# First group in 64-row transposes and 128x64 product tiles, state products moved, and other homes and queue places for the weight pieces of an mLSTM + SwiGLU kernel

## The chip, the cores and the metric

The kernel runs on one core of one Trainium2 chip. The metric is the device time of one execution in microseconds (us).

## The reference

An mLSTM cell over 4 batches, 8 heads, 768 steps and head size 40, then a SwiGLU feed-forward block over the 3072 resulting tokens (320 features, 1536 hidden):

```python
for t in range(S):                      # per batch and head
    m_new  = maximum(f[t] + m, i[t])
    f_stab, i_stab = exp(f[t] + m - m_new), exp(i[t] - m_new)
    C = f_stab * C + i_stab * outer(v[t], k[t])
    n = f_stab * n + i_stab * k[t]
    y[t] = sigmoid(o[t]) * (C @ q[t]) / maximum(abs(n @ q[t]), 1)
x   = y as (B*S, H*D) = (3072, 320)
out = (silu(x @ w_gate) * (x @ w_val)) @ w_out
```

q, k, v, the gates and the output are float32. The three weight matrices reach the kernel as 64-bit floats, so that a weight is two 32-bit words in DRAM.

## The kernel before, in words

**Groups.** The 768 steps are cut into six groups of 128 tokens (for 4 batches a group is 512 tokens). Group 0 has no earlier state and is computed in a form of its own (the functions named `first_...`). Later groups work in half groups of 64 tokens with a state `C` kept in `C_ring`. The core runs group 0's cell, then the feed-forward of group 0 while the cell of group 1 is prepared between its blocks, and so on.

**Order.** The scheduling is manual: every engine executes its instructions in the order in which the program writes them, and waits where an input or a buffer is not ready. That holds for DMA issues too: `nc.sync.dma_start` stands in SyncE's order (SP in the profile), `nc.scalar.dma_start` in ScalarE's (ACT). A wait therefore holds up all that stands behind it on the same engine. `A`, `V` and `G` stand for ScalarE, VectorE (DVE) and GpSimd (POOL).

**Group 0's cell (lines 599 to 646).** The heads are handled in two halves P = 0 and 1 (two batches u each). The decay weights of the first 128 steps are built in PSUM by three rounds of matmuls (L512, L516, L521) and go through Exp into `W0` (a view of `h_sb[:, 0:8]`). `first_turn` transposes k and q (128x128 tiles, L541), `first_scores` multiplies them (L551) and DVE multiplies the scores into `W0` (L555). `first_own(u)` multiplies `W0` with the values (L562), `first_x` divides by the normaliser, `sig` applies Sigmoid to the output gate `o_sb` on ACT, `first_gate` multiplies it in. `first_seam` transposes x into `xT` for the feed-forward (L596), and `first_state` (L584) makes the state that group 1 starts from. `burn` (L501) is matmuls without use. PSUM tiles come from two rings of four banks each, "cell" and "gen".

**Weight pieces.** `PIECES` numbers ten loads, p0 to p9. p0 and p1 hold the gate and value weights of one block of 128 hidden features, p2 to p6 those of two blocks (p2: blocks 2 and 3, ... p5: 8 and 9, p6: 10 and 11), each in three DMAs: one for the gate half (640 KB in p2 to p6) and two for the value half (512 and 128 KB). p7 to p9 hold `w_out`, 1280 KB each, in blocks 12 to 17. `piece_load` puts the raw words into a buffer of the ring `raw` (two buffers) or into a borrowed home. `convert(j)` turns a block into float32 in three steps: `scale(j)` (two ACT instructions, L211 and L213), `join(j)` (two DVE instructions, L220 and L221), and `rounded(j)` (L228, on POOL or DVE).

**Feed-forward of group 0.** `hidden(0, m)` is one block of 128 hidden features: 20 matmuls (`gv_ps`, L683), then the conversions that `ahead[m]` names, then Silu on ACT (L688) and a product on DVE (L689) that frees the two PSUM banks. Those matmuls use two of the four "gen" banks, so that block m + 2 needs the product of block m to be done. `ahead` converts block j at an earlier m: block 7 and 8 at m = 5, 9 at 6, 10 at 7, 11 at 8. After block m the functions in `slots[m]` are called: the loads of group 1's k, q, v, the sums over the later gates (`late_sums`, `late_maxima`, `late_decay`), a store of the maxima `M_sb` to a DRAM tile `M_dram`, and `weights_load(1)`, two loads of `M_dram` spread over partitions into `w_sb`. From slot 7 on `w_sb` becomes group 1's decay weights: `weights_sub` on DVE (L483), `weights_mask` on POOL (L488), `weights_exp` on ACT (L492), then the product with the scores (`weigh`, L359) and the state sums on TensorE (`add`, L378).

The core of `hidden`, which sets the order of steps that the change leaves alone:

```python
for kc in range(NKC): ...               # 20 matmuls L683
for f in first:                         # the conversions of ahead[m]
    f()
nc.scalar.activation(sg, ps[0], AF.Silu)
nc.vector.tensor_tensor(hid(g, m), sg, ps[1], op=ALU.mult)
```

Of the kernel before, what the change touches and what calls it, by code (L numbers as in the profile page):

```python
# [14 lines left out]
ALU = mybir.AluOpType  # L15
# [9 lines left out]
def kernel(  # L25
# [50 lines left out]
    def bank(name, tag="cell"):  # L76
        return psum.tile([128, 512], F32, name=name, tag=tag)
# [61 lines left out]
    def copy(eng, dst, src):  # L139
        if eng is nc.scalar:  # L140
            nc.scalar.copy(dst, src)
        else:
            eng.tensor_copy(dst, src)
# [16 lines left out]
    def piece_load(p, home=None):  # L160
        kind, m, n = PIECES[p]
        if kind == "gv":
            a, d = NKC, n * 128
            gate_w, val_w = (w[:, m * 128:(m + n) * 128].rearrange("(c p) f -> p c f", p=HP) for w in (moe_w_gate, moe_w_val))
            src = [(slice(0, HP), slice(0, NKC), gate_w), (slice(HP, 128), slice(0, NKC - 1), val_w[:, 1:]),
                   (slice(HP, 128), slice(NKC - 1, NKC), val_w[:, 0:1])]
            queues = (nc.sync,) + 2 * (nc.scalar if p < 5 else nc.sync,)
        else:
            a, d = n, DM
            src = [(slice(0, 128), slice(0, n), moe_w_out[m * 128:(m + n) * 128].rearrange("(a p) d -> p a d", p=128))]  # L170
            queues = (nc.sync,)
        if src[0][2].dtype == F32:
            for r, cs, w in src:
                if kind == "o":
                    nc.sync.dma_start(out=wo_sb[r, m:m + n, :], in_=w)
                else:
                    for x in range(n):
                        nc.sync.dma_start(out=wgv_sb[r, m + x, cs], in_=w[:, :, ts(x, 128)])
            return
        if home is None:  # L180
            raw = conv.tile([128, 4 * NKC * 128], U32, name="raw")
        else:
            raw = home.rearrange("p a t -> p (a t)").bitcast(U32)
        raw = raw[:, 0:2 * a * d]
        for (r, cs, w), queue in zip(src, queues):
            queue.dma_start(out=raw[r].rearrange("p (a d) -> p a d", a=a)[:, cs], in_=w.bitcast(U32))
        words = raw.rearrange("p (a d two) -> p a d two", two=2, a=a)
        raws[p] = (words[:, :, :, 0], words[:, :, :, 1])
        split(p)
# [40 lines left out]
    def convert(j, eng=None):  # L230
        scale(j)
        join(j)
        rounded(j, eng)
# [41 lines left out]

    M0 = early.tile([128, L], F32)
    M_of = wo_sb.rearrange("p m d -> p (m d)")[:, 0:H * L].rearrange("p (h t) -> p h t", t=L)
    M_sb = early.tile([BH, NS - 2, SUB], F32)
    m_in = early.tile([BH, NS - 2, 1], F32)
    step1 = keep1  # L280
# [13 lines left out]
    def late_sums():  # L294
        nc.vector.tensor_tensor_scan(flat(f_sb), flat(keep1), flat(f_sb), 0.0, op0=ALU.mult, op1=ALU.add)
        nc.gpsimd.memset(step1, 0.0)
        nc.gpsimd.tensor_sub(i_sb, i_sb, f_sb)
# [11 lines left out]
    M_dram = tc.dram_tile([BH, S - L], F32, name="M_dram")  # L309


    def turn_one(P, src, dst, engs):
        tp = [bank("tp_kq").rearrange("p (a t) -> p a t", t=SUB) for _ in range(2)]
        for a in range(UA):
            h = P * UH + 2 * a
            for i in range(2):
                nc.tensor.transpose(tp[i][:, a, :], src[half(i), h:h + 2, :].rearrange("p h d -> p (h d)"),
                                    ident[half(i), half(i)])
        for i in range(2):
            copy(engs[i], dst[:, P * UA:(P + 1) * UA, half(i)], tp[i])  # L320
# [139 lines left out]
    def xT(n):  # L460
        return xT_sb
# [36 lines left out]
    def burn(n, tag="cell"):  # L498
        t = bank("burn", tag)
        for _ in range(n):  # L500
            nc.tensor.matmul(t, lhsT=junk[:, 0:128], rhs=junk, start=True, stop=True)  # L501
# [29 lines left out]
    def first_values(P):  # L531
        nc.gpsimd.tensor_copy(w_end[:, heads(P)], W0[:, heads(P), end])
        nc.gpsimd.tensor_tensor(vw_sb[:, heads(P)], v_sb[:, heads(P)], w_end[:, heads(P)].to_broadcast([128, UH, D1]),
                                op=ALU.mult)

    def first_turn(P, src, dst, engs):
        for b in range(2):
            tp = bank("tp_kq").rearrange("p (a t) -> p a t", t=L)
            for a in range(UA // 2):
                h = P * UH + b * H + 2 * a  # L540
                nc.tensor.transpose(tp[:, a, :], src[:, h:h + 2, :].rearrange("p h d -> p (h d)"), ident)  # L541
            a = P * UA + b * UA // 2
            copy(engs[b], dst[:, a:a + UA // 2, :], tp)

    def first_scores(P):
        for b in range(2):
            sp = [bank("sp").rearrange("p (a t) -> p a t", t=L) for _ in range(2)]
# [11 lines left out]
    def first_own(u):  # L559
        first_y[u] = bank("first_y", "gen")[:, 0:H * D1].rearrange("p (h d) -> p h d", d=D1)  # L560
        for h in range(H):
            nc.tensor.matmul(first_y[u][:, h, :], lhsT=W0[:, u * H + h, :], rhs=v_sb[:, u * H + h, :], start=True, stop=True)  # L562

    def first_x(u):
        y = first_y.pop(u)
        den = work.tile([128, UH, 1], F32, name="den")[:, 0:H]
        nc.vector.tensor_scalar(den, y[:, :, D:], scalar1=1.0, scalar2=None, op0=ALU.max)
        nc.vector.scalar_tensor_tensor(den, in0=y[:, :, D:], scalar=-1.0, in1=den, op0=ALU.mult, op1=ALU.max)
        nc.vector.reciprocal(den, den)
        nc.vector.tensor_tensor(x_sb[:, u, 0:DM].rearrange("p (h d) -> p h d", d=D), y[:, :, 0:D],  # L570
                                den.to_broadcast([128, H, D]), op=ALU.mult)

    def first_gate(P):
        for u in (2 * P, 2 * P + 1):
            x = x_sb[:, u, 0:DM].rearrange("p (h d) -> p h d", d=D)
            nc.vector.tensor_tensor(x, x, o_sb[:, u * H:(u + 1) * H], op=ALU.mult)
        nc.gpsimd.tensor_copy(x_sb[:, 2 * P:2 * P + 2, DM:], x_sb[:, 2 * P:2 * P + 2, 0:HP])

    def first_state(P, tag="cell"):
# [7 lines left out]
    def first_kept(P, ps, eng):  # L587
        copy(eng, state(2)[:, P * UA:(P + 1) * UA], ps)

    def first_seam(P, engs):  # L590
        for c, eng in zip(range(0, NKC, 2), engs):
            cs = range(c, min(c + 2, NKC))
            tp = bank("tp_x")[:, 0:len(cs) * 2 * L].rearrange("p (c u s) -> p c u s", u=2, s=L)
            for w in cs:
                for b in range(2):
                    nc.tensor.transpose(tp[:, w - c, b, :], x_sb[:, 2 * P + b, ds(w * HP, 2 * HP)], ident)  # L596
            copy(eng, xT(0)[:, c:c + len(cs), 2 * P * L:(2 * P + 2) * L].rearrange("p c (u s) -> p c u s", u=2), tp)

    burn(7)
    banks = [(u, j) for j in range(2) for u in range(B)]  # L600
    for f in (first_mask, first_inputs, first_maxima):
        for u, j in banks:
            f(u, j)
    first_exp(0)
    first_turn(0, k_sb, kT, (V, V))
    first_turn(0, q_sb, qT, (A, V))
    first_exp(1)
    first_values(0)
    first_scores(0)
    first_own(0)  # L610
    late_sums()
    first_turn(1, k_sb, kT, (A, A))
    first_x(0)
    first_turn(1, q_sb, qT, (A, V))
    load(o_sb, o_gate, 0, 1)
    piece_load(0)
    first_own(1)
    first_values(1)
    first_scores(1)
    first_x(1)  # L620
    sig(0)
    piece_load(1)
    burn(3)
    first_own(2)
    piece_load(2, h_sb[:, 1:1 + NKC])
    sig(1)
    burn(2)
    first_own(3)
    first_gate(0)
    first_x(2)  # L630
    first_x(3)
    first_gate(1)
    first_seam(0, (A, A, V))
    scale(0)
    ps1 = first_state(1, "gen")
    burn(1, "gen")
    piece_load(3, h_sb[:, NH - NKC:])
    join(0)
    first_seam(1, (A, A, V))
    rounded(0, V)  # L640
    first_kept(0, first_state(0), A)
    first_kept(1, ps1, V)
    convert(1, V)
    nc.scalar.activation(warm, warm, AF.Silu)
    piece_load(4, wo_sb)
    piece_load(5)


    pair = early.tile([BH, PP], F32)
# [279 lines left out]
    def load_all(dst, a, n):  # L929
        for P in range(2):  # L930
# [7 lines left out]
    ahead[0] = []  # L938
    ahead.update({4: [6], 5: [7, 8], 6: [9], 7: [10], 8: [11], 9: [], 10: [], 11: []})
    slots = {  # L940
        0: [run(convert, 2, V), run(late_maxima), run(load_all, k_sb, k, 1),
            run(nc.sync.dma_start, out=M_dram, in_=flat(M_sb)), run(load_all, q_sb, q, 1)],
        1: [run(piece_load, 6), run(late_decay)],
        2: [run(nc.scalar.activation, step1, step1, AF.Exp), run(decay_rows), run(weights_load, 1), run(load_all, v_sb, v, 1)],
        3: [run(late_turns)],
        4: [run(decay)],
        5: [run(turn, 0, (A, A), (A, V))],
        6: [run(turn, 1, (A, A), (A, V)), run(piece_load, 7)],
        7: [run(weights_sub, 1, 0), run(weights_mask, 0), run(weights_sub, 1, 1), run(weights_mask, 1), run(nc.gpsimd.memset, q_sb, 0.0)],
        8: [run(weights_exp, 0), run(weights_exp, 1), run(weigh_values, G, 0), run(weigh_values, G, 1),  # L950
# [124 lines left out]
```

## Time and profile before

| | |
|---|---|
| time, median of 3 runs | 517.14 us (514.86 to 517.34) |
| the profiled execution's own time | 516.62 us |
| its span in the profile | 514.8 us |
| granted TensorE clock | 0.998 |
| busy PE / DVE / ACT / POOL | 506.3 / 345.3 / 179.7 / 279.2 us |
| share of the 16 DMA engines over the span, SP's queue | 47.7% |

The span counts from the program's first instruction to its last; the 1.8 us between it and the execution's time lie outside. Group 0's cell takes the first 31.6 us, the twelve blocks of its hidden layer run from there to 92.7 us. Durations below come from this one execution. A busy PE means that matmuls are in flight, and idle time of an engine costs only where something later waits for it. In the DMA parts, "landing" is the time from the issue of a transfer to its completion. In a window's row, the DMA share is the mean over the 16 DMA engines and passes 1 where packets overlap.

### The profile page before, as it was taken

The page shows a single profiled execution, that of the slowest core. Times are in us where ns is not written, and L with a number is a line of the kernel's source. Part 1 is how long each engine was busy: PE and PEld are TensorE (multiplying, and loading weights), DVE is VectorE, ACT ScalarE, POOL GpSimd, SP SyncE. Part 2 cuts the span into 40 slices and gives each one's busy share as a digit, 9 for nine tenths or more (in the row PEclk, how much of TensorE's full clock was granted, in tenths as well). Part 3 has the DMA queues.
Part 4 walks back from the last instruction along what each step waited for, and adds up shares of the span by engine and source line. Part 5 has one row for each costly group of instructions (what it writes and reads, how often), then busy time and mean ns, then how long its engine had stood idle before and what let it go on. Part 6 is the DMA issues. An engine that isn't in the chain of part 4 may idle for free.

```text
span 514.8 us, 14725 instructions
## 1 busy us (share of the span) xinstructions
PE 506.3 (98%) x6309; PEld 430.3 (84%) x6309; DVE 345.3 (67%) x547; ACT 179.7 (35%) x269; POOL 279.2 (54%) x283
## 2 busy tenths in 40 slices
PE   8999999999999999999999999999999999999997
PEld 4964445667888889898899898999898899988896
DVE  5779666899858879857669656659666754233421
ACT  3377555434222244322335322345231330123210
POOL 1303327566399789457657457657347750166710
PEclk9999999999999999999999999999999999999999
DMA  9999999698100866700886600896700210100001
GB/s 126 176 241 221 171 215 216 148 180 94 52 3 12 153 101 76 105 3 6 132 127 76 107 3 3 122 138 77 108 4 1 34 21 20 33 1 1 0 14 39
DMA packets 205497, 43.28 MB, mean 84 GB/s; under 512 B 193432, under 2 KB 200600, under 8 KB 205432
## 3 DMA queue, kind: packets, MB, share of 16 engines
q1 hardware_dynamic: 203444, 39.49, 47.7%
q10 hardware_dynamic: 1988, 2.85, 2.4%
q8 instruction: 50, 0.82, 0.7%
q14 instruction: 15, 0.12, 0.1%
HBM read 35.68 MB, written 4.01 MB: 77 GB/s over the span
## 4 chain that ended last, share of the span: by engine, by line
PE 77%; DVE 11%; POOL 4%; issue 3%; DMA 2%; ACT 2%; SPq 1%; DVEq 0%; ACTq 0%; POOLq 0%
PE gv_x L831 23%; PE o_ps L754 20%; PE gv_y L831 18%; PE gv_ps L683 5%; DMA w_sb<-M_dram 2%; PE inter L401 2%; PE intra L406 2%; PE sp L352 2%; PE first_y L562 1%; POOL w_sb L488 1%; PE burn L501 1%; DVE vw_sb L419 1%; POOL tmp L872 1%; PE tp_kq L541 1%; PE sp L551 1%
## 5 line engine op out<-in xcount | busy, mean ns | idle before, releaser
L831 PE MATMUL gv_x<-xT,wgv_sb 64*128 64x256 f32 x720 | 93.7, 382 | 0.7 <-ACT tmp L881 0.4
L831 PEld LDWEIGHTS gv_x<-xT,wgv_sb 64*128 64x128 f32 x720 | 69.0, 187 | 9.0 <-issue 1.1
L754 PE MATMUL o_ps<-wo_sb,h_sb 128*128 128x160 f32 x480 | 67.4, 300 | 0.0
L754 PEld LDWEIGHTS o_ps<-wo_sb,h_sb 128*128 128x128 f32 x480 | 65.6, 190 | 1.7 <-issue 1.7
L683 PE MATMUL gv_ps<-xT,wgv_sb 64*128 64x512 f32 x240 | 53.5, 595 | 0.3 <-DVE wgv_sb L228 0.3
L488 POOL TENSOR_SCALAR_AFFINE_SELECT w_sb<-w_sb 64x1024 f32<-64x1024 f32 x20 | 31.1, 1555 | 25.3 <-DVE w_sb L483 16.8
L683 PEld LDWEIGHTS gv_ps<-xT,wgv_sb 64*128 64x128 f32 x240 | 23.5, 187 | 25.0 <-issue 23.5
L831 PE MATMUL gv_y<-q_sb,wgv_sb 64*128 64x256 f32 x360 | 44.1, 377 | 0.3 <-DVE x_sb L871 0.3
L831 PE MATMUL gv_y<-xT,wgv_sb 64*128 64x256 f32 x360 | 44.0, 376 | 0.0
L879 ACT ACTIVATE h_sb<-gv_x 128x256 f32<-128x256 f32 x30 | 11.5, 384 | 86.3 <-PE gv_x L831 86.2
L831 PEld LDWEIGHTS gv_y<-q_sb,wgv_sb 64*128 64x128 f32 x360 | 35.3, 187 | 4.2 <-DVE x_sb L871 0.7
L831 PEld LDWEIGHTS gv_y<-xT,wgv_sb 64*128 64x128 f32 x360 | 35.5, 187 | 3.4
L754 PE MATMUL o_ps<-wT,S 128*128 128x160 f32 x240 | 33.5, 300 | 0.1
L754 PEld LDWEIGHTS o_ps<-wT,S 128*128 128x128 f32 x240 | 32.8, 190 | 0.4 <-DVE tmp L768 0.4
L871 DVE TENSOR_TENSOR tmp<-tmp,gv_y 128x1024 f32<-128x1024 f32 x15 | 18.3, 1220 | 20.2 <-PE gv_y L831 18.3
L872 POOL TENSOR_TENSOR tmp<-tmp 128x512 f32<-128x512 f32 x15 | 20.0, 1335 | 21.1 <-DVE tmp L871 21.1
L831 PE MATMUL gv_x<-q_sb,sw 64*128 64x256 f32 x240 | 31.0, 376 | 0.0
L852 POOL TENSOR_TENSOR h_sb<-tmp 128x512 f32<-128x512 f32 x13 | 16.7, 1287 | 25.5 <-ACT tmp L851 25.5
L871 DVE TENSOR_TENSOR x_sb<-x_sb,gv_y 128x1024 f32<-128x1024 f32 x15 | 18.3, 1218 | 17.0 <-PE gv_y L831 16.1
L861 ACT COPY tmp<-gv_x 128x1024 f32<-128x1024 f32 x15 | 15.2, 1012 | 40.5 <-PE gv_x L831 40.5
L721 POOL TENSOR_TENSOR S<-h_sb 128x256 f32<-128x256 f32 x30 | 22.8, 759 | 9.2 <-DVE h_sb L852 7.3
L723 POOL TENSOR_TENSOR S<-S,h_sb 128x256 f32<-128x256 f32 x30 | 27.3, 911 | 0.0
(216 smaller groups left out, 1004.2 us busy)
## 6 DMA issues: line engine op xcount, KB each, us to landing
w_sb<-M_dram SPq DMA_DIRECT2D x10, 512.0 KB, 7.3
k_sb<-in_k_dram SPq DMA_DIRECT2D x12, 320.0 KB, 6.5
v_sb<-in_v_dram SPq DMA_DIRECT2D x12, 320.0 KB, 5.8
o_sb<-in_o_gate_dram SPq DMA_DIRECT2D x12, 320.0 KB, 6.3
raw<-in_moe_w_out_dram SPq DMA_DIRECT2D x3, 1280.0 KB, 7.6
x_sq<-k_sb SPq DMA_DIRECT2D x64, 40.0 KB, 2.0
q_sb<-in_q_dram SPq DMA_DIRECT2D x32, 64.0 KB, 2.5
out_dram<-tmp SPq DMA_DIRECT2D x24, 80.0 KB, 2.8
```

Source lines behind the costliest of these rows:

```text
L352: nc.tensor.matmul(sp[two][half(i), a, :], lhsT=kT[feats(two), P * UA + a, half(i)], rhs=qT[feats(two), P * UA + a, half(i)], start=True, ...
L488: nc.gpsimd.affine_select(w, w, compare_op=ALU.is_ge, fill=NEG, base=0, pattern=[[0, UH], [1, SUB]], channel_multiplier=-1)
L683: nc.tensor.matmul(ps[i], lhsT=wgv_sb[half(i), m, kc, :], rhs=x[half(i), kc, :], start=(kc == 0), stop=(kc == NKC - 1))
L721: eng.tensor_tensor(S1[:, k], lo[:, second_half], hi[:, second_half], op=ALU.add)
L723: eng.tensor_tensor(S2[:, k], S1[:, k], lo[:, first_half], op=ALU.subtract)
L754: nc.tensor.matmul(node[x][:, i], lhsT=lhs(k)[:, ts(i, L)], rhs=rhs(k), start=start and k == 0 and i == 0, stop=stop and k == KH - 1, skip ...
L831: nc.tensor.matmul(ps[:, i, cols], lhsT=lhs(c)[half(i)], rhs=rhs(c)[half(i)], start=start and c == 0, stop=stop and c == n - 1, skip_group ...
L852: (nc.vector if k == KH - 1 else nc.gpsimd).tensor_tensor(h_sb[:, 2 * k + 1], uw[:, 0], uw[:, 1], op=ALU.mult)
L861: nc.scalar.copy(uw, x)
L871: nc.vector.tensor_tensor(uw, uw, y, op=ALU.add)
L872: nc.gpsimd.tensor_tensor(uw[:, :, second_half], uw[:, :, second_half], uw[:, :, first_half], op=ALU.add)
L879: nc.scalar.activation(h[:, first_half], x[:, 0, first_half], AF.Silu)
```

## The change

Group 0's transposes of k, q and x use the functions of the later groups (`turn_one`, `seam`): two tiles of 64 tokens in place of one of 128, with twice the instructions. `first_own` does each head's product as two tiles of 64 output tokens. Both turns and scores come before `first_own(0)`. The state products of both halves stand together between the two seams, and the three later `burn` calls are gone. The output gate of the first half is multiplied in on POOL, the seam's evictions are spread differently over ACT and DVE, and `late_sums` comes after `convert(1)`.

Piece p2 goes to a part of `wo_sb` that nothing uses yet, p4 into the ring `raw` with all its DMAs on SP, and p5 and p6 move to slots 1 and 4. `late_maxima` and the store of `M_dram` move from slot 0 to 1, `late_decay` from slot 1 to 2. SP's order of transfers from p4 on changes from "p4 p5 k k M_dram q q p6 w_sb w_sb v v p7" to "p4 k k q q p5 M_dram w_sb w_sb v v p6 p7".

```diff
-            queues = (nc.sync,) + 2 * (nc.scalar if p < 5 else nc.sync,)
+            queues = (nc.sync,) + 2 * (nc.scalar if p < 4 else nc.sync,)
...
+    spare_wo = wo_sb.rearrange("p m d -> p (m d)")[:, H * L:H * L + 4 * NKC * 128].rearrange("p (a t) -> p a t", a=1)
...
-    def turn_one(P, src, dst, engs):
-        tp = [bank("tp_kq").rearrange("p (a t) -> p a t", t=SUB) for _ in range(2)]
+    def turn_one(P, src, dst, engs, tag="cell"):
+        tp = [bank("tp_kq", tag).rearrange("p (a t) -> p a t", t=SUB) for _ in range(2)]
...
         for h in range(H):
-            nc.tensor.matmul(first_y[u][:, h, :], lhsT=W0[:, u * H + h, :], rhs=v_sb[:, u * H + h, :], start=True, stop=True)
+            for i in range(2):
+                nc.tensor.matmul(first_y[u][half(i), h, :], lhsT=W0[:, u * H + h, half(i)], rhs=v_sb[:, u * H + h, :],
+                                 start=True, stop=True)
...
-    def first_gate(P):
+    def first_gate(P, eng):
...
-            nc.vector.tensor_tensor(x, x, o_sb[:, u * H:(u + 1) * H], op=ALU.mult)
+            eng.tensor_tensor(x, x, o_sb[:, u * H:(u + 1) * H], op=ALU.mult)
...
     first_exp(0)
-    first_turn(0, k_sb, kT, (V, V))
-    first_turn(0, q_sb, qT, (A, V))
+    turn_one(0, k_sb, kT, (V, V))
+    turn_one(0, q_sb, qT, (A, V))
     first_exp(1)
     first_values(0)
     first_scores(0)
-    first_own(0)
-    late_sums()
-    first_turn(1, k_sb, kT, (A, A))
-    first_x(0)
-    first_turn(1, q_sb, qT, (A, V))
+    turn_one(1, k_sb, kT, (A, A))
+    turn_one(1, q_sb, qT, (A, V))
     load(o_sb, o_gate, 0, 1)
     piece_load(0)
+    first_own(0)
     first_own(1)
     first_values(1)
+    first_x(0)
     first_scores(1)
-    first_x(1)
     sig(0)
     piece_load(1)
-    burn(3)
+    first_x(1)
     first_own(2)
-    piece_load(2, h_sb[:, 1:1 + NKC])
+    first_own(3)
+    piece_load(2, spare_wo)
+    first_gate(0, G)
     sig(1)
-    burn(2)
-    first_own(3)
-    first_gate(0)
+    seam(0, 0, (A, A, A, A))
     first_x(2)
     first_x(3)
-    first_gate(1)
-    first_seam(0, (A, A, V))
+    first_gate(1, V)
     scale(0)
-    ps1 = first_state(1, "gen")
-    burn(1, "gen")
+    states = [first_state(P, "gen") for P in range(2)]
     piece_load(3, h_sb[:, NH - NKC:])
     join(0)
-    first_seam(1, (A, A, V))
+    seam(0, 1, (A, V, A, V))
     rounded(0, V)
-    first_kept(0, first_state(0), A)
-    first_kept(1, ps1, V)
+    first_kept(0, states[0], A)
+    first_kept(1, states[1], V)
     convert(1, V)
+    late_sums()
     nc.scalar.activation(warm, warm, AF.Silu)
-    piece_load(4, wo_sb)
-    piece_load(5)
+    piece_load(4)
...
     slots = {
-        0: [run(convert, 2, V), run(late_maxima), run(load_all, k_sb, k, 1),
-            run(nc.sync.dma_start, out=M_dram, in_=flat(M_sb)), run(load_all, q_sb, q, 1)],
-        1: [run(piece_load, 6), run(late_decay)],
-        2: [run(nc.scalar.activation, step1, step1, AF.Exp), run(decay_rows), run(weights_load, 1), run(load_all, v_sb, v, 1)],
+        0: [run(convert, 2, V), run(load_all, k_sb, k, 1), run(load_all, q_sb, q, 1)],
+        1: [run(piece_load, 5), run(late_maxima), run(nc.sync.dma_start, out=M_dram, in_=flat(M_sb))],
+        2: [run(late_decay), run(nc.scalar.activation, step1, step1, AF.Exp), run(decay_rows), run(weights_load, 1), run(load_all, v_sb, v, 1)],
         3: [run(late_turns)],
-        4: [run(decay)],
         5: [run(turn, 0, (A, A), (A, V))],
+        4: [run(decay), run(piece_load, 6, spare_wo)],
```

`first_turn` and `first_seam` are removed. The functions that replace them, `turn_one` and `seam`, were there for the later groups.

More of the change, by code (lines that the diff above doesn't have):

```diff
@@ L534, in first_values @@
                                 op=ALU.mult)
[L536 to L543, printed above, removed]
     def first_scores(P):
@@ L588, in first_kept @@
         copy(eng, state(2)[:, P * UA:(P + 1) * UA], ps)
[L590 to L597, printed above, removed]
     burn(7)
```

## The prediction

> **What bounds the kernel now.** I read the page first, then the chain that ended last, in order of time, then the timeline of each engine over the first 135 us, and last the transfers with their times to landing. Only the first 90 us matter: nothing behind them is edited. The windows view of the stretch after the first cell:
>
> ```profile
> core 0: us, PE busy (x) PEld busy (x) DVE busy (x) ACT busy (x) POOL busy (x), PEclk, DMA share, GB/s
> 36.00:46.00 10.00, 10.00 (x48) 4.88 (x46) 8.73 (x15) 6.77 (x10) 1.55 (x1) 1.00 1.06 276
> 46.00:52.00 6.00, 6.00 (x36) 2.94 (x34) 5.30 (x12) 5.96 (x8) 3.10 (x2) 1.00 1.18 166
> 52.00:61.00 9.00, 9.00 (x70) 4.50 (x68) 6.00 (x10) 5.07 (x10) 3.73 (x3) 1.00 1.17 159
> 61.00:67.50 6.50, 6.50 (x60) 3.51 (x58) 3.85 (x6) 4.17 (x9) 0.91 (x1) 1.00 1.12 210
> 67.50:76.00 8.50, 8.50 (x44) 3.86 (x42) 6.04 (x7) 4.75 (x7) 1.91 (x1) 1.00 1.01 190
> ```
>
> PE never rests and the DMA share never falls below 1.0: both are full. So a transfer's landing is set by what stands ahead of it in SP's order. From SP's timeline (start, us):
>
> ```profile
> 53.20 2.63 SPq L137 DMA_DIRECT2D q_sb<-in_q_dram  x2
> 55.94 1.99 SPq L186 DMA_DIRECT2D raw<-in_moe_w_gate_dram  x1
> 57.97 1.28 SPq L186 DMA_DIRECT2D raw<-in_moe_w_val_dram  x2
> 59.35 7.34 SPq L479 DMA_DIRECT2D w_sb<-M_dram  x2
> 66.73 5.16 SPq L137 DMA_DIRECT2D v_sb<-in_v_dram  x2
> ```
>
> The two lines of L186 are p6. By their times to landing, q's last load is there at 60.9, p6 at 67.15 (58.63 + 8.5), `w_sb` at 70.4 and 72.7, and the trace's landing events put the second v load at 75.6. Who needs them, from the timelines of ACT and DVE:
>
> ```profile
> 67.25 0.79 ACT L211 ACTIVATE top<-raw 128x640 f32<-128x640 f32 x1 [0.42 <-DMA raw<-in_moe_w_val_dram]
> 70.11 0.60 ACT L688 ACTIVATE tmp<-gv_ps 128x512 f32<-128x512 f32 x1 [1.39 <-PE gv_ps L683]
> 70.74 0.69 DVE L689 TENSOR_TENSOR h_sb<-tmp,gv_ps 128x512 f32<-128x512 f32 x1 [0.35 <-ACT tmp L688]
> 72.79 2.36 DVE L483 TENSOR_TENSOR w_sb<-g_T,w_sb 128x1024 f32<-128x1024 f32 x2 [1.36 <-DMA w_sb<-M_dram]
> ```
>
> This is the place to remember. `scale(10)` at 67.25 already waits 0.42 us for p6, and block 7's Silu (70.11) and product (70.74) stand behind it on the same two engines; `weights_sub` (72.79) waits for `w_sb` alone. From there the chain that ended last runs on, mask by mask, without slack:
>
> ```profile
> 74.09 2.07 POOL w_sb L488
> ...
> 85.69 1.29 DVE w_sb L359 x2
> 87.02 1.14 PE add L378 x62
> ```
>
> PE waits 0.3 us for that DVE product at 85.8. Whatever moves the start of `weights_sub` later therefore moves the end by as much.
>
> **Part 1: the first cell's PE work.** Old and new forms both stand in this trace, the new ones in group 1:
>
> ```profile
> 9.87 1.09 PE L541 MATMUL tp_kq<-ident,k_sb 128*128 128x128 f32 x8
> 59.24 0.66 PE L317 MATMUL tp_kq<-ident,k_sb 64*128 64x64 f32 x16
> 22.67 1.87 PE L562 MATMUL first_y<-v_sb,h_sb 128*128 128x41 f32 x16
> 27.73 1.13 PE L584 MATMUL add<-vw_sb,k_sb 128*64 128x41 f32 x32
> 29.03 1.25 PE L596 MATMUL tp_x<-ident,x_sb 128*128 128x128 f32 x10
> 109.16 0.84 PE L471 MATMUL tp_x<-ident,x_sb 64*128 64x64 f32 x20
> ```
>
> Four turns save 1.09 - 0.66 = 0.43 us each, four `first_own` 0.74 each, two seams 0.41 each, the six burns 0.2 each: 1.7 + 3.0 + 0.8 + 1.2 = 6.7 us of PE. Little of it is on the path. q's second half lands at about 17.2 us (the old turn of it began at 17.31), and with `first_own(0)` now behind that turn PE waits there and reaches the second scores at about 20.0 (before: 20.09); DVE's products follow until 23.7 as before. `first_own(3)` ends at about 24.9 in place of 26.7. But the start of block 0 at 31.62 waits for `xT` and for `rounded(0)`, and these hang on ACT: `sig(1)` starts at 26.33 because p2's last value DMA, ahead of it in ACT's order, is issued only at 25.79, when p0's gate half has landed (25.7). That order stays, and p2's new home does not lift it. Behind `sig(1)` (to 27.1) come now four evictions on ACT (0.75 us for two in group 1, so 1.5; before 1.07 for two), hence `scale(0)` from 28.6 (before 28.14), `join(0)` from 29.4 (0.49 + 0.82), two evictions on DVE (0.88; before 0.42) and `rounded(0)` (0.81): block 0 starts at about 32.5, **+0.9 us**. The gate on POOL costs about 0.65 us each by L429 (1.27 for 640 elements), done by 25.9 under `sig(1)`; without that cover, 0.9 against DVE's 0.44. The states (two of 1.1 us between the seams) end at 29.0 under `scale(0)` and `join(0)`. Bounds on this start: -0.7 (ACT's order relaxes) to +1.5.
>
> `late_sums` (1.47 on DVE) goes to about 35 to 36.5, still ahead of Silu(0); `late_decay` moves to slot 2 ahead of Exp on ACT and of the ten small transposes (0.8 us) at 49.2, a wait of 0 to 1 us of PE. All this counts only if nothing later is the limit.
>
> **Part 2: the queue.** Three weights-of-two-blocks pieces change places, and everything stays on a full queue, so sums can be made from landings.
>
> p4: it was on two queues. p5 and p6, on SP alone, took 6.1 us (45.6 to 51.7) and 6.2 (60.9 to 67.15); p3 and p4, on two queues, 3.9 (to 40.5) and 5.0 (to 45.6). Moving p4 wholly to SP costs 0 to 2.3 us; I take 0.6, since ACT's queue still carries p2 and p3 for most of that time. The Trainium skill ("DMA: Bandwidth & Descriptors", "Rules for kernel authors") says that transfers to disjoint partition halves serialize on the same engines whether one queue issues them or two. By that the 0.6 would be nothing; the 5.0 against 6.1 speaks a little against it.
>
> p5: behind k k q q (9.2 us from 51.7 to 60.9, the small `M_dram` store with them) it lands at about 45.6 + 0.6 + 9.2 + 6.1 = 61.5 in place of 51.7. `scale(8)` began at 57.38; now at 61.6, so Silu(5) ends at about 63.8 and its product at 64.5. Block 7, which needs those banks, began at 65.57: covered by 1 us, and a wait of some tenths if that cover is gone. The turns of slot 6 may wait another 0 to 1 us for evictions queued behind Silu(5).
>
> p6: `w_sb` and v (75.6 - 67.15 = 8.5 us) now stand ahead of it. And `M_dram` is directly ahead of `w_sb`, which reads it: SP holds the `w_sb` issue until the store has landed, with nothing else behind it to feed the engines (before, q q p6 lay between). The trace of before shows no such wait. Below, it is 0, if p5's tail covers it; above, one store and one start from an idle queue, 2.8 (output stores of group 1 and later) + 2.0 (the copies of `k_sb`), 4.8. I take 2.5, the middle, as the tail covers part. So p6 lands at T = 67.15 + 8.5 + 0.6 + 2.5 = 78.75, bounds 75.65 to 82.75. It is not issued ahead of SP's order, since its place in slot 4 is behind `weights_load(1)` of slot 2.
>
> **Where the stall goes.** `scale(10)` still stands ahead of Silu(7) on ACT, and `join(10)` and `rounded(10)` ahead of the product on DVE. In the trace, `rounded(10)` ended 3.2 us after p6's landing (70.38 - 67.15). Then come the product, 0.69, and `weights_sub`: it starts at T + 3.9 = 82.7 in place of 72.79. That is **+9.9 us**. Block 9 on PE needs the banks of block 7, so PE stands still from about 75 to 82.7. Behind it the order on DVE, POOL and ACT is as before (subtraction, `convert(11)`, masks, Exp, `weigh`, `add`), so the chain keeps its 13.0 us from L483 to `add`. The +0.9 of part 1 and the waits at blocks 5 and 6 are swallowed by that gap, as p6's landing does not depend on them. p7 lands about 6 us behind p6 (85), and `scale(12)` would be at 93: no second stall.
>
> Sum against the profiled execution: 516.6 + 9.9 = **526.5 us**. The median of the runs shown is 0.5 above this execution, which I leave out.
>
> **Rivals.**
> *p6 in time.* If the queue had room that the shares hide and p6 landed before 69 (T + 3.9 = 72.8), only part 1 and small waits remain: 516.6 + 0.9 = 517.5, no difference; this ends on the other side and is decided by that one landing. For it: k, q and `w_sb` come earlier, so the stall on `w_sb` goes (PE waits of 0.3 us). Against it: the share of 1.0 and more in every stretch to 76 us. Chance 0.10.
> *The cell's PE saving arrives.* If ACT's `sig(1)` comes free early, `first_own(3)` being 1.8 us earlier counts, and with p6 in time and PE's small waits gone some 3 us fall away: 513.6. It needs both; 0.08.
> *A partial stall.* T between 70 and 74, because v and `w_sb` overlap with p6 on the engines: +1 to +5, about 520. Landings come in the order of issue in this trace, which speaks against it. Chance 0.08.
> *The stall cools the clock.* PE has no wait over 1.2 us in the first 135 us and the granted clock is 1.00 in every row, so no row shows what a gap of 7 us does. If block 9 (4.4 us) and the scores behind it (2.0) ran at half the clock, `add` would start not at T + 16.9 but at about T + 21, behind PE: 4 us more, 530.5. Chance 0.12. The Trainium skill ("TensorE: Matmul & The Clock Gate", Part 1) has the clock halved after an idle window of about 3.4 us and back after as long a busy one; by that, about 1.7 us are lost, most of it under DVE's chain.
>
> **How the numbers follow.** The forecast has 0.62 (T between its bounds: 523.4 to 530.5), and with the cooled clock and the partial stall the slower side has 0.82. Faster by over 0.5% (2.6 us, about what a measurement of this kernel can tell) has 0.08, and within 0.5% 0.10. The likeliest case's own range is 523 to 530.5. The stall's bounds leave some tenths of its chance outside, so the range takes in the rival without stall: 517 to 531.
>
> **What would show it.** Right: SP's timeline with p6 behind v; `scale(10)` idle for 9 us or so on "DMA" (the waits of ACT name the tile of the new home, `wo_sb`); a gap of 7 us on PE before block 9; L483 at about 82 to 83; an `M_dram` store followed by a hole in the DMA share near 62 us; block 0 starting at 32 to 33. Wrong: L211 of block 10 before 70, or a PE without gap between 70 and 85; then the queue was not what set p6's landing. If block 0 starts below 31, the ACT order of part 1 was read wrongly.

## The result, and the profile after

The changed kernel takes **530.19 us** (median; 529.86 to 531.37) against 517.01 for the kernel before (514.86 to 517.34): a ratio of 1.027 with the interval 1.0247 to 1.0293, so 13.2 us slower. The forecast was 526.5, its range 517 to 531. The profiled execution has a span of 528.1 us, 13.3 above that of before. Two executions far above the others of their kernels are left out of all that follows: one of e9 (596.65 us at a granted clock of 0.85) and one of the kernel before (2082.1 us).

Lines of the page of the changed kernel: the busy tenths of PE, the granted clock and the DMA engines in 40 slices of 13.2 us.

```profile
PE   8869995999999999999999999999999999999997
...
PEclk9789997999999999999999999999999999999999
DMA  9999899279800288810297900288900110100001
```

PE has a hole in the seventh slice (79 to 92 us) and one in the third (26 to 40 us), and the clock falls about both. From 105 us on PE and the clock look as before. The timeline of SP shows the new order of transfers (start, us):

```profile
52.80 2.30 SPq L186 DMA_DIRECT2D raw<-in_moe_w_gate_dram  x1
55.15 1.28 SPq L186 DMA_DIRECT2D raw<-in_moe_w_val_dram  x2
56.52 0.53 SPq L914 DMA_DIRECT2D M_dram<-M_sb  x1
64.57 2.06 SPq L480 DMA_DIRECT2D w_sb<-M_dram  x2
66.72 6.00 SPq L137 DMA_DIRECT2D v_sb<-in_v_dram  x2
72.81 1.62 SPq L186 DMA_DIRECT2D wo_sb<-in_moe_w_gate_dram  x1
74.48 1.27 SPq L186 DMA_DIRECT2D wo_sb<-in_moe_w_val_dram  x2
```

The store of `M_dram` is issued at 56.5, and SP issues nothing until 64.57: `w_sb` waits for the store's landing (64.55). The last two lines are p6, now behind v. Its consumers, from the timelines of ACT, DVE and PE:

```profile
83.63 0.77 ACT L211 ACTIVATE top<-wo_sb 128x640 f32<-128x640 f32 x1 [11.76 <-DMA wo_sb<-in_moe_w_val_dram]
84.98 0.59 ACT L669 ACTIVATE tmp<-gv_ps 128x512 f32<-128x512 f32 x1
86.67 0.68 DVE L670 TENSOR_TENSOR h_sb<-tmp,gv_ps 128x512 f32<-128x512 f32 x1
87.27 2.35 DVE L484 TENSOR_TENSOR w_sb<-g_T,w_sb 128x1024 f32<-128x1024 f32 x2
85.62 7.43 PE L664 MATMUL gv_ps<-xT,wgv_sb 64*128 64x512 f32 x20 [6.21 <-ACT tmp L669]
95.01 4.56 PE L664 MATMUL gv_ps<-xT,wgv_sb 64*128 64x512 f32 x20
100.29 2.33 PE L379 MATMUL add<-vw_sb,k_sb 64*64 64x41 f32 x126 [0.29 <-DVE w_sb L360]
```

These are the lines of the kernel before, moved. `scale(10)` waits 11.76 us for p6 (before 0.42), block 7's Silu and product follow it, and `weights_sub` (now L484) starts at 87.27 in place of 72.79: 14.5 us later, with nothing of its own to wait for (no bracket; `w_sb` had landed at 73.45). PE stands idle for 6.2 us before block 9. `add` is 14.5 us late too (100.29 against 85.82). About 1 us of it comes back by the next seam (122.65 against 109.16, so 13.5): a wait of PE at the `intra` products that no releaser explains was 1.15 us before and is 0.19 now.

### The profile page after: what moved, and what is told of

The parts are those of the page before. It is cut to its first block, busy times and chain, and to the rows that moved or that the text cites. A ratio compares the mean times of both kernels' runs of the same rounds, so it can differ in the third digit from the quotient of the medians.

```text
span 528.1 us, 14949 instructions
## 1 busy us (share of the span) xinstructions
PE 507.8 (96%) x6419; PEld 428.3 (81%) x6419; DVE 343.0 (65%) x545; ACT 179.5 (34%) x271; POOL 281.1 (53%) x285
## 4 chain that ended last, share of the span: by engine, by line
PE 66%; DVE 10%; issue 5%; POOL 4%; DMA 3%; ACT 2%; SPq 0%; DVEq 0%; ACTq 0%; POOLq 0%
PE gv_x L812 22%; PE o_ps L735 20%; PE gv_y L812 17%; PE inter L402 2%; PE intra L407 2%; PE sp L353 2%; DMA M_dram<-M_sb 2%; POOL w_sb L489 1%; DMA w_sb<-M_dram 1%; PE gv_ps L664 1%; DVE x_sb L436 1%; DVE vw_sb L420 1%; POOL tmp L853 1%; DVE w_sb L484 1%; POOL h_sb L833 1%
## 5 line engine op out<-in xcount | busy, mean ns | idle before, releaser
L664 PE MATMUL gv_ps<-xT,wgv_sb 64*128 64x512 f32 x240 | 58.0, 623 | 9.3 <-ACT tmp L669 6.2
L812 PEld LDWEIGHTS gv_y<-q_sb,wgv_sb 64*128 64x128 f32 x360 | 35.3, 187 | 3.7 <-DVE x_sb L852 0.3
```

The costliest lines, as they stand in the source:

```text
L664: nc.tensor.matmul(ps[i], lhsT=wgv_sb[half(i), m, kc, :], rhs=x[half(i), kc, :], start=(kc == 0), stop=(kc == NKC - 1))
L812: nc.tensor.matmul(ps[:, i, cols], lhsT=lhs(c)[half(i)], rhs=rhs(c)[half(i)], start=start and c == 0, stop=stop and c == n - 1, skip_group ...
```

## Experiments

All were compared with the kernel before on their own chip (medians 515.8 to 516.3), and a time "over before" is taken against that. The kernel before scatters by 3 us on one chip (514.4 to 517.9) and its medians lie between 515.8 and 517.0, so a difference between two runs' medians is good to about 1 us.

**e1: the changed cell with the pieces of before.**

```diff
-            queues = ... (nc.scalar if p < 4 else nc.sync,)
+            queues = ... (nc.scalar if p < 5 else nc.sync,)
-    piece_load(2, spare_wo)
+    piece_load(2, h_sb[:, 1:1 + NKC])
-    piece_load(4)
+    piece_load(4, wo_sb)
+    piece_load(5)
     slots 0 to 4 as before the change
```

> The changed kernel with the pieces, their homes, their queues and the slots 0 to 4 of before; the first cell stays changed (64-row transposes, product tiles, moved states, no late burns). Theory (p6's landing holds block 7's Silu and with it the decay weights): p6 lands at 67 to 70 again, L483 starts at 73 to 77, no gap on PE before block 9; what is left is the later start of block 0 (35.3 in place of 31.6), so 518 to 521. Rival (the cell and its cooled clock carry most of the loss): 524 or more, PE late already at block 9.

519.68 us (518.05 to 521.86), ratio 1.0073 (1.0047 to 1.0099). p6 landed at 67.46, `weights_sub` started at 74.74, and PE passes blocks 7 to 9 in one run:

```profile
33.48 19.15 PE L665 MATMUL gv_ps<-xT,wgv_sb 64*128 64x512 f32 x80 [3.21 <-ACT low L213]
68.97 13.10 PE L665 MATMUL gv_ps<-xT,wgv_sb 64*128 64x512 f32 x60
```

The cell by itself costs about 3.4 us over before, not 13 (the trace is of an execution of 518.05 us, 1.6 below the median). Block 0 started at 33.48, not at 35.3, so part of its delay belongs to the pieces.

**e2: the cell of before with the changed pieces**, the same edits the other way round.

> The kernel before with the pieces, homes, queues and slots 0 to 4 of the changed one; the first cell is that of before. Theory: p6 lands at 81 to 84, scale(10) waits about 10 us for it, L483 starts at 85 to 88, time 527 to 531 although block 0 starts at 31.6. Rival (cell): at most 521.

529.25 us (528.43 to 530.05), ratio 1.025 (1.022 to 1.0279): 13.0 over before. `scale(10)` waited 10.96 us for p6 and `weights_sub` started at 86.26, as in the changed kernel:

```profile
82.62 0.77 ACT L211 ACTIVATE top<-wo_sb 128x640 f32<-128x640 f32 x1 [10.96 <-DMA wo_sb<-in_moe_w_val_dram]
```

The transposes, the product tiles and the missing burns have no visible share in the loss, as long as the pieces stand so. One thing was not expected: block 0 started at 35.23 although the cell was that of before.

**e3: the store ahead of p5.**

```diff
-        1: [run(piece_load, 5), run(late_maxima), run(nc.sync.dma_start, out=M_dram, ...)],
+        1: [run(late_maxima), run(nc.sync.dma_start, out=M_dram, ...), run(piece_load, 5)],
```

> The changed kernel with late_maxima and the store of M_dram ahead of p5 in slot 1 in place of behind it. Theory: the store has landed when SP comes to w_sb, so the hole of some 3 us on the queue near 65 us goes, p6 lands at about 80.5 in place of 83.6, and the time falls by 3 to about 527. Rival (the hole is only displaced, since w_sb, v and p6 are limited by their own packets): 530, p6 at 83 to 84.

527.28 us, ratio 1.0218 (1.0189 to 1.0247), 2.9 less than the changed kernel (2.2 less when each is taken over before). SP issued `w_sb` at 58.32, right behind p5, `scale(10)` began at 80.40 in place of 83.63 and `weights_sub` at 84.04. Without the hole on the queue `weights_sub` starts 3.2 us earlier, and 2 to 3 us of that reach the end.

**e4: blocks 10 and 11 converted later**, the transfers untouched.

```diff
-    ... 6: [9], 7: [10], 8: [11], 9: [], ...
+    ... 6: [9], 7: [], 8: [], 9: [10, 11], ...
```

> The changed kernel with block 10 and 11 converted in hidden 9 in place of hidden 7 and 8; all transfers as in the changed kernel. Theory (the loss is not that block 10 comes late but that its scale stands ahead of Silu(7) on ACT): p6 lands at 83.6 as before, but Silu(7) runs at about 75, L483 at 76 to 78 behind w_sb, PE passes block 9 without a gap and waits shortly for block 10; time 520 to 523. Rival (PE needs block 10's data, so its landing is the limit wherever the conversion stands): 528 to 530.

525.34 us, ratio 1.0171 (1.0145 to 1.0198): 4.9 less than the changed kernel, where 7 to 10 were expected. The timelines of PE and DVE:

```profile
70.67 13.10 PE L664 MATMUL gv_ps<-xT,wgv_sb 64*128 64x512 f32 x60
89.47 6.72 PE L664 MATMUL gv_ps<-xT,wgv_sb 64*128 64x512 f32 x20 [3.67 <-DVE wgv_sb L228]
76.45 2.36 DVE L484 TENSOR_TENSOR w_sb<-g_T,w_sb 128x1024 f32<-128x1024 f32 x2
```

`weights_sub` starts at 76.45 and block 9 has no gap before it, as the theory has it. But then block 10 has to wait for its data (3.67 us on `rounded(10)`) and, after that gap, takes 6.72 us in place of 4.56, which here nothing covers: `add` follows at once at 96.12. So both readings hold a part. Taking `scale(10)` out of Silu(7)'s way gives back 4 to 5 us (4.9 by the medians, 4.1 over before). The rest is not the landing alone: p6 landed at 82.87, `scale(10)`, now behind `weights_exp` on ACT, began at 84.41, and `join(10)` and `rounded(10)` took 4.2 us (85.23 to 89.41) where they took 2.3 in the changed kernel (84.43 to 86.75). The late data, this slower conversion and the lowered clock are not told apart.

**e5: p6 ahead of `w_sb`.**

```diff
-        1: [run(piece_load, 5), run(late_maxima), run(nc.sync.dma_start, out=M_dram, ...)],
+        1: [run(late_maxima), run(nc.sync.dma_start, out=M_dram, ...), run(piece_load, 5), run(piece_load, 6, spare_wo)],
-        4: [run(decay), run(piece_load, 6, spare_wo)],
+        4: [run(decay)],
```

> The changed kernel with the order of transfers alone mended: late_maxima, the store of M_dram, p5 and p6 all in slot 1, in this order, so that p6 stands ahead of w_sb and v again. Everything else as changed (homes, p4 on SP, late p5, first cell). Theory (p6's place on the queue sets the time): p6 lands at 70 to 72, scale(10) waits little, w_sb lands at 75 to 77, L483 at 76 to 77.5, no gap on PE before block 9, time 519 to 522. Rival (homes and queues of p4 and p5 cost as much): 525 or more.

520.4 us (519.74 to 521.59), ratio 1.008 (1.0054 to 1.0105). p6 landed at 70.56 and was waiting when `scale(10)` came to it:

```profile
73.12 0.81 ACT L211 ACTIVATE top<-wo_sb 128x640 f32<-128x640 f32 x1
```

`w_sb` landed at 76.58, `weights_sub` started at 77.76, right behind block 7's product. Changing the order of transfers gives 9.8 us of the changed kernel's time back (8.7 over before), with homes, queues and cell as changed. Of the 4.4 us over before that remain, the trace shows PE late: block 0 started at 35.34, its first four blocks took 20.30 us (17.61 before), and block 7's Silu waited for PE until 76.53.

**e6: `sig(1)` ahead of p2's DMAs on ACT.**

```diff
-    piece_load(2, spare_wo)
-    first_gate(0, G)
     sig(1)
+    piece_load(2, spare_wo)
+    first_gate(0, G)
```

> The changed kernel with sig(1) ahead of piece_load(2) in ACT's order. Theory (block 0's start is swallowed by the gap before block 9, since p6's landing does not depend on it): sig(1) starts 2 to 4 us earlier than 29.3, block 0 at 33 to 34.5 in place of 35.3, p6 still at 83 to 84, time 529.5 to 531, no change. Rival (the later start of block 0 passes through to the end): 1 to 3 us less, 527 to 529.

530.06 us, ratio 1.0265 (1.0236 to 1.0294): no change in time, but block 0 did not start earlier either; it started at 36.67. `sig(1)` ran at 24.99, and then ACT's timeline shows where the wait went:

```profile
27.33 3.59 ACTq L186 DMA_DIRECT2D wo_sb<-in_moe_w_val_dram  x2
30.97 1.41 ACT L141 COPY xT<-tp_x 128x512 f32<-128x512 f32 x4 [5.24 <-DMA raw<-in_moe_w_gate_dram]
33.83 2.16 ACTq L186 DMA_DIRECT2D h_sb<-in_moe_w_val_dram  x2
```

The `ACTq` lines are p2's and p3's value DMAs. Their issue takes until 30.9 and 36.0, and the evictions of the two seams (from 30.97 and 36.03) stand behind them. As a test of whether block 0's start reaches the end, this run therefore says little: the start moved 1.4 us the other way and the time stayed.

**e7: e1 with burns in PE's waits.**

```diff
     turn_one(1, k_sb, kT, (A, A))
+    burn(6, "gen")
...
+    burn(3)
     first_own(2)
+    burn(2)
     first_own(3)
...
     seam(0, 1, (A, V, A, V))
+    burn(8, "gen")
```

> Run e1 (changed cell, pieces of before) with burns put where PE waits: 6 behind the second turn of k, 3 and 2 ahead of the last two first_own, 8 behind the second seam. Theory (the cell is slower because PE's clock falls in its waits): granted clock 1.0 throughout, the second scores 2.1 us in place of 3.5, block 0 at 32.5 or earlier, time 516.5 to 518.5. Rival (ACT's order sets block 0's start, the clock only shortens PE's wait for it): block 0 at 33 to 33.5, 519 to 520 as in e1.

516.6 us (515.93 to 517.24), ratio 1.0013 (1.0 to 1.0027). The clock was 1.00 in every stretch. Block 0 still started at 33.60, as the rival said, but the first four blocks took 17.57 us in place of e1's 19.15:

```profile
33.60 17.57 PE L669 MATMUL gv_ps<-xT,wgv_sb 64*128 64x512 f32 x80 [1.38 <-ACT low L213]
```

So the theory's result came by another way than it said: without burns e1 lost its clock in the first blocks and not in the cell, where its second scores took 2.06 us already. And with the clock kept, a block 0 that starts 2 us later than before ends at the same time: `w_sb` landed only at 72.1, and `weights_sub` started at 73.29, 0.5 us later than before.

**e8: the kernel before with p4 on one queue.**

```diff
-            queues = ... (nc.scalar if p < 5 else nc.sync,)
+            queues = ... (nc.scalar if p < 4 else nc.sync,)
```

> The kernel before with p4's two value DMAs on SP in place of ACT; nothing else. Theory (one queue alone moves a piece slower, so that all behind p4 lands later): p4 lands at 47 to 48.3 in place of 45.6, p6 and w_sb 1.5 to 2.5 us later, L483 at 74 to 75, time 518 to 519.5. Rival (both queues feed the same engines, so it makes no difference): p4 at 45.6 to 46.3, time 516 to 517.3.

518.25 us (515.48 to 520.29), ratio 1.0041 (1.0017 to 1.0065). p4's last part landed at 47.6 in place of 45.6, p6 at 70.1, `w_sb` at 75.29, and `weights_sub` started at 75.39, 2.6 later than before and bound by that landing. The trace is of an execution of 520.2 us, 2 above the median, so these landings may be later than the usual ones. Part of the 2 us is not rate: the first value DMA was issued only at 36.37, when p2's gate half had landed (36.35), where ACT had issued it at 31.64.

**e9: burns in PE's gap before block 9**, 28 of them behind slot 8 of the changed kernel.

> The changed kernel with 28 burns (about 6 us) between block 8 and block 9, in the gap of PE. Theory (the stall cools the clock, block 9 takes 7.4 us in place of 4.5, but the chain over DVE, POOL and ACT stands until 94.9 and covers it): granted clock 1.0 from 80 to 95 us, block 9 in 4.5 us, L483's chain and block 10's start at 94 to 95 unchanged, time 529 to 531. Rival (the cooled clock reaches the end): 526.5 to 528.

Three executions gave 530.31 to 530.66, ratio 1.0281 (1.0239 to 1.0322). There is no trace of them, so that the clock in the gap and block 9's duration are not shown; the time is that of the changed kernel.

**e10: e2 with p2 and p3 issued behind the second seam.**

```diff
-    piece_load(2, spare_wo)
...
-    piece_load(3, h_sb[:, NH - NKC:])
...
     first_seam(1, (A, A, V))
+    piece_load(2, spare_wo)
+    piece_load(3, h_sb[:, NH - NKC:])
```

> Run e2 (cell of before, pieces of the changed kernel) with the loads of p2 and p3 issued behind the second seam, so that no DMA issue stands ahead of sig(1), the seams' evictions and scale(0) on ACT. Theory (block 0 starts late because ACT, with value DMAs in its order, waits for landings of earlier transfers): sig(1) starts at 25 in place of 29.7, block 0 at 31.5 to 32.5 in place of 35.2; p6 stays late, so the time stays at 528 to 531. Rival (block 0 waits for the weights of p0 or for PE): block 0 at 34 or later.

529.95 us, ratio 1.0272 (1.0231 to 1.0314). Block 0 started at 32.19, 3 us earlier than in e2, and block 1 then waited, because ACT was held behind the seam instead of ahead of it:

```profile
32.19 4.56 PE L683 MATMUL gv_ps<-xT,wgv_sb 64*128 64x512 f32 x20 [0.28 <-DVE wgv_sb L228]
41.52 15.89 PE L683 MATMUL gv_ps<-xT,wgv_sb 64*128 64x512 f32 x60 [4.77 <-DVE wgv_sb L228]
85.30 8.50 PE L683 MATMUL gv_ps<-xT,wgv_sb 64*128 64x512 f32 x20 [2.74 <-ACT tmp L688]
```

This run answers what e6 could not. PE loses 4.8 us more before block 1, the gap before block 9 shrinks from 6.8 (e2) to 2.7, and the end stays within 1 us. While p6 is late, a loss of this size on PE ahead of block 9 does not reach the end.

## Why the prediction was right, and where its sizes were off

**The mechanism** held at each step that the sum rests on: p6 behind `w_sb` and v, `scale(10)` waiting ahead of Silu(7), `weights_sub` late, the chain behind it unchanged (13.0 us from L484 to `add`, as before). From p6's landing to `weights_sub` it took 3.8 us, where 3.9 was reckoned. e2 shows that the pieces alone do it, e5 that the places of p6 and of the store on the queue are some 9 us of it.

**The term that was mis-sized is T**, p6's landing: about 83.5 in place of 78.75, just above its upper bound of 82.75. With that T the prediction's own sum gives 516.6 + 14.6 = 531.2 us, outside its range of 517 to 531. The time landed inside because about 1 us comes back behind `add`, which the prediction did not have: that the range held is in part luck. By the landings in the trace of the changed kernel:

| part of the queue | reckoned, us | measured, us |
|---|---|---|
| p4 landed at | 46.2 | 48.3 |
| k k q q | 9.2 | 10.9 (to 59.2) |
| p5 | 6.1 | 5.3 (to 64.5, the store with it) |
| hole, and the first `w_sb` load | 2.5 + 3.2 | 6.3 (to 70.9) |
| second `w_sb` load, v v | 5.2 | 5.4 (to 76.3) |
| p6 | 6.2 | 7.1 |

p4 is the largest miss. I reckoned with its rate on one queue; its issue was late as well, at 38.39, just after p3's gate half had landed (38.31). The hole (3.1 us by the difference of 6.3 and 3.2) was well placed between its bounds, and `weights_sub` starts 3.2 us earlier without it (e3). A rate of 2.3 us for a k or q load, taken from one stretch, was 2.7 here. p6 took 0.9 us more than reckoned in this execution; behind the same second v load it took 6.5 us in e2, 6.2 in e4 and 6.5 in e6, so most of that is scatter.

**Part 1** had the right verdict, since nothing of it counts at the end, and a wrong number: block 0 at 35.27 in place of 32.5, above the bound. The sentence that failed is "That order stays, and p2's new home does not lift it". The order stayed, but the landings that ACT's issues wait for did not. `sig(1)` waited until 29.26, for p1's gate half (28.71), and p3's value DMAs, ahead of the second seam's evictions, were issued only at 33.31, when p2's gate half had landed (33.29). e2 has the same delay with the old cell, and e10, with ACT free, starts block 0 at 32.19. The wait for q's second half ("PE waits there") came as said, 1.39 us on its landing, but PE's clock fell with it, which the prediction did not have: the first two `first_own` took 3.64 us together (2.07 in e1), and the second scores started at 21.77 in place of 20.0 and took 3.48 us in place of 2.06.

**The 6.7 us of PE saved** in tiles and burns were rightly put off the path. Burns can be worth more than they cost: without any in these places the median of e1 is 3 us above that of e7. But e7 has 19 of them, partly in other places than the six that the change took out, so what those six were worth is not shown. The new tile forms cost what the rows of the kernel before said where the clock was full (32 products of `first_own` 1.13 us in e7).

**The clock rival** came true in its cause and not in its price. The windows view of the changed kernel:

```profile
85.00:90.00 5.00, 4.38 (x10) 1.79 (x12) 4.86 (x6) 3.82 (x6) 1.44 (x1) 0.54 1.08 363
90.00:95.00 5.00, 5.00 (x142) 2.98 (x138) 4.74 (x4) 1.06 (x1) 4.82 (x4) 1.00 0.69 91
```

The granted clock (the third number from the end) falls to 0.54, and block 9 takes 7.43 us. Block 10 starts at 95.01, when both the scores on PE and block 8's product on DVE (94.23 + 0.68) are just done, so the 2.9 us are covered, if only just. e9 agrees by its time alone; in e4, where PE was on the path behind its gap, block 10 paid 2.2 us. The Trainium skill ("TensorE: Matmul & The Clock Gate", Part 1) lets the clock halve after an idle window of about 3.4 us. The gap of 6.2 us agrees with that. In the first cell the clock fell at 18 us although PE's waits before it were only 1.04, 0.41 and 1.39 us, so here the measurement decides: several short waits can come before a fall.

**The rule of the Trainium skill on queues**, that disjoint halves serialize whether one queue issues them or two ("DMA: Bandwidth & Descriptors", "Rules for kernel authors"), would by itself have e8 equal to the kernel before. e8 was some 2 us slower, p4 2 us later. Since the issue moved too, e8 doesn't separate rate from issue; what it shows is that moving p4 to one queue was not free here.

**What stays open**: how far p4's lateness in the changed kernel is rate and how far issue, and how the 4.4 us that e5 keeps divide between homes, queues and the cell. None of the runs beat the kernel before; the nearest, e7, is not told apart from it, and its trace says why: `w_sb` lands at 72.1 us, against 72.7 before.

## What to carry to other kernels

Where the DMA queue is full, read a transfer's landing off what stands ahead of it in its queue, and then look at what stands behind its consumer on the consumer's engine: the loss is made there. A store that the next load reads wants something else between them on the queue (a hole of 3 us here). A DMA issue placed in a compute engine's order can hold that engine until an earlier transfer has landed (ACT was idle for 7.34 us before `sig(1)` here). So look at what stands behind it on that engine: in e10 the issues moved behind the second seam, block 0 started 3 us earlier, and block 1 waited 4.8 us.

## What the runs showed of the hardware

- In these programs an issue waited for the landing of an earlier transfer that it has no data in common with: ACT's issues at 26.85, 28.73 and 33.31 us stand 0.02 us behind the landings at 26.83, 28.71 and 33.29 of p0's, p1's and p2's gate halves. The transfers of the trace share eight landing marks in rotation; which earlier transfer p2's and p3's value DMAs wait for changed with the pieces (e2) and not with the cell (e1). That the rotation is the cause is read from the trace, not tried.
- In the changed kernel the granted clock was 0.50 from 18 to 24 us, after waits of PE of 1.04, 0.41 and 1.39 us. In e1, with the same cell and waits of 1.04, 0.33 and 0.38 us, it stayed at 1.00 there. e1's clock fell only around a wait of 3.21 us (0.84 from 32 to 34 us, 0.50 from 34 to 36); e7, whose burns left 1.38 us of that wait, kept it at 1.00.
- The load of `w_sb`, which reads the store, was issued 0.02 us behind the store's landing (64.57 against 64.55). From 64 to 67 us the DMA share was 0.28, between 0.79 in the 4 us ahead and 1.12 in the 3 us behind:

```profile
64.00:67.00 3.00, 3.00 (x44) 1.83 (x41) 1.58 (x3) 2.46 (x5) 0.82 (x2) 1.00 0.28 64
```
